# Moving regroup copies, sums and stores between engines in a linear-attention and feed-forward kernel

## The chip, the cores and the metric

The kernel runs on one core of a Trainium2 chip. The metric is the device time of one execution in microseconds (us), as the median of several runs. The core has five engines that run at the same time and wait for one another by semaphores: TensorE (PE, matrix products into the accumulator memory PSUM), VectorE (DVE), ScalarE (ACT), GpSimd (POOL), which here does copies and sums and issues the loads, and SyncE (SP), which here issues the stores. Each engine takes its own instructions in the order in which the kernel lists them.

## The reference: attention without softmax, then a feed-forward layer

```python
# q, k, v: 8 batches x 8 heads x 576 positions x 64, float32
kv  = einsum('bhsd,bhse->bhde', k, v)
att = einsum('bhsd,bhde->bhse', q, kv)
att = att / sqrt(mean(att * att, axis=-1) + 1e-6) * g_norm
x   = att.transpose(0, 2, 1, 3).reshape(4608, 512)
h   = x @ w_in                                   # 4608 x 2048
g   = maximum(h, 0) + alpha * minimum(h, 0)
out = g @ w_out                                  # 4608 x 512
```

## The kernel before

The 4608 tokens are handled in nine windows of 512 (window 0 to 8). All products are in float16 with sums in float32. While window w goes through its first layer, the attention steps of window w+1 are mixed in, and so is the second layer of window w-1.

**Loads and regroup copies.** Pool loads a batch in float16 into a staging tile. The products need k and q in another order, and a copy makes it, on Pool for batches 2 to 7 (batch 0 and 1 are copied by VectorE).

```python
def regroup(b, nm, h0, h1, eng=None):
    dst = bufs[b % NBUF][nm][:, 0:TPP, h0:h1, :].rearrange("p t h d -> p h t d")
    src = stages[b, nm][:, h0:h1, :, :]
    ...
        (eng or nc.vector).tensor_copy(out=dst, in_=src)          # L148
def regroup_batch(b):
    for nm in ("k", "q"):
        regroup(b, nm, 0, H, nc.gpsimd)
```

**Attention steps**, for four pairs of heads in each window: "t" transposes q on TensorE and copies it out of PSUM, "kv" makes the product of k and v and masks it, "ot" multiplies both and squares, "ssq" sums the squares and normalises. The results of "t" and "kv" use the same PSUM bank by turns.

```python
def step_t(b, j, pool=(ps_s, "s")):
    ...                                                           # 5 transposes, L236
    nc.vector.tensor_copy(out=qts[b, j][:], in_=qt_ps[:, 0:S])    # L245
def step_kv(b, j, pool=(ps_s, "s")):
    ...                                                           # 5 products, L251
    nc.vector.tensor_mul(out=kvs[b, j][:], in0=kv_ps[:], in1=mask32[:])   # L259
```

**First layer.** A unit of a window is one block of 128 of the 2048 columns: four products (L332), a Relu on ScalarE (L339) and a combining operation on VectorE (L343), which gives gt. A window has 16 units.

**Second layer.** For window 0 it is a plain product. From window 1 on, the four quarters of the product are computed with seven products instead of eight, from sums of activations and of weights. The activation sums s1 to s4 are made for four groups of blocks:

```python
def s_sum(w, n, k):          # a11, a21, a12, a22: quarters of the activations
    if n == 1:   nc.vector.tensor_add(out=t[:], in0=a21, in1=a22)
    elif n == 2: nc.vector.tensor_sub(out=t[:], in0=sums[w, 1, k][:], in1=a11)
    elif n == 3: nc.gpsimd.tensor_sub(out=t[:], in0=a11, in1=a21)             # L421
    else:        nc.gpsimd.tensor_sub(out=t[:], in0=a12, in1=sums[w, 2, k][:])  # L423

def w_sums(i):               # i = 0, 1; VectorE, 128x1024 each, L400 to L403
    nc.vector.tensor_sub(out=t1, in0=w_lo(i, HC, D_MODEL), in1=w_lo(i, 0, HC))
    nc.vector.tensor_sub(out=t2, in0=w_hi(i, HC, D_MODEL), in1=t1)
    nc.vector.tensor_sub(out=t4, in0=w_hi(i, 0, HC), in1=t2)
    nc.vector.tensor_sub(out=w_lo(i, HC, D_MODEL),
                         in0=w_hi(i, HC, D_MODEL), in1=w_lo(i, HC, D_MODEL))

Y_ORDER = (1, 6, 2, 7, 5, 4, 3)     # order of the seven products, 16 matmuls each (L460)
```

Product 6 reads s2, product 7 reads s3 and the fourth weight sum, product 5 reads s1, product 3 reads s4. They collect in three PSUM banks X, Y and Z; y_read (L472 to L485) adds banks and partial results together, giving the quarters c11, c22, c21 and c12, each stored when it is ready.

**The order of a window**, with what is listed for Pool in it:

```python
for w in range(1, NW):
    if 1 < w and w + 2 < B:
        load_batch(w + 2)
        regroup_batch(w + 2)                 # waits for the loads just issued
    for u in range(NF):
        if w == 1 and u == first_g - 1:      # first_g is 4 in window 1
            load_batch(3)
            regroup_batch(3)
        m1_group(w, G_ORDER[u])
        unit_sums(w, u)                      # s1, s3 and s2, s4 of a group every four units
        if w > 1 and u < 2:
            unit_sums(w - 1, NF + u)         # the last group of the window before
        ...                                  # 7 matmuls of the second layer of w-1
            if w == 1 and u == NF - 1:
                w_sums(0); w_sums(1)
        ...                                  # attention steps of w+1
```

Of the kernel before, what the change touches and what calls it, by code (L numbers as in the profile page):

```python
# [9 lines left out]
FP32 = mybir.dt.float32  # L10
FP16 = mybir.dt.float16
# [6 lines left out]
def kernel(  # L18
# [11 lines left out]
    nc = tc.nc  # L30
# [124 lines left out]
# [3 lines that stand above are left out]
# [74 lines left out]
    def step_t(b, j, pool=(ps_s, "s")):  # L232
        qs = pair_cols(b, "q", j)
        qt_ps = pool[0].tile([P, NT * P], FP16, name="qt_ps", tag=pool[1])
        for t in range(NT):
            nc.tensor.matmul(  # L236
                out=qt_ps[:, t * P : (t + 1) * P],
                lhsT=qs(t),
                rhs=ident16[:],
                is_transpose=True,  # L240
                start=(t == 0),
                stop=(t == NT - 1),
            )
        qts[b, j] = attn_p.tile([P, S], FP16, name="qt_sb", tag=f"qt{j}")
        nc.vector.tensor_copy(out=qts[b, j][:], in_=qt_ps[:, 0:S])  # L245

    def step_kv(b, j, pool=(ps_s, "s")):
        ks, vs = pair_cols(b, "k", j), pair_cols(b, "v", j)
# [107 lines left out]
    def y_mm(y, w, a, g):  # L356
# [2 lines left out]
            start=(g == 0), stop=(g == NF - 1),  # L359
        )  # L360

    def store_rows(n0, src, c0, c1):
        i = 0
        while i < P:
            b, r = divmod(n0 + i, S)
            if r < MAIN:
                t, p = divmod(r, P)
                cnt = min(P - i, P - p)
                rows = out[b * S : b * S + MAIN, :].rearrange("(p t) m -> t p m", t=TPP)
                dst = rows[t, p : p + cnt, c0:c1]  # L370
            else:
                cnt = min(P - i, S - r)
                dst = out[b * S + r : b * S + r + cnt, c0:c1]
            nc.sync.dma_start(out=dst, in_=src[i : i + cnt])
            i += cnt

    def y_out(y, w, a):
# [10 lines left out]
    def w_lo(i, c0, c1):  # L388
        return w_out_sb[i][:, :, c0:c1]

    def w_hi(i, c0, c1):
        return w_out_sb[i + WQ // 2][:, :, c0:c1]

    def w_sums(i):
        sl = slice(i * GW, (i + 1) * GW)
        for n in (1, 2, 4):
            if n not in wsum:
                wsum[n] = w_p.tile([P, NK, HC], FP16, name=f"wsum{n}")
        t1, t2, t4 = (wsum[n][:, sl, :] for n in (1, 2, 4))
        nc.vector.tensor_sub(out=t1, in0=w_lo(i, HC, D_MODEL), in1=w_lo(i, 0, HC))  # L400
        nc.vector.tensor_sub(out=t2, in0=w_hi(i, HC, D_MODEL), in1=t1)
        nc.vector.tensor_sub(out=t4, in0=w_hi(i, 0, HC), in1=t2)
        nc.vector.tensor_sub(  # L403
            out=w_lo(i, HC, D_MODEL), in0=w_hi(i, HC, D_MODEL), in1=w_lo(i, HC, D_MODEL),
        )

    sums = {}
    HW = W // 2
# [1 line left out]
    def s_sum(w, n, k):  # L410
        lo, hi = gts[w, k], gts[w, k + KQ]
        a11, a21 = lo[:, :, 0:HW], lo[:, :, HW:W]
        a12, a22 = hi[:, :, 0:HW], hi[:, :, HW:W]
        t = sum_p.tile([P, 2, HW], FP16, name=f"s{n}", tag=f"s{n}{k}", bufs=1 if n == 2 else 2)
        sums[w, n, k] = t
        if n == 1:
            nc.vector.tensor_add(out=t[:], in0=a21, in1=a22)
        elif n == 2:
            nc.vector.tensor_sub(out=t[:], in0=sums[w, 1, k][:], in1=a11)  # L419
        elif n == 3:  # L420
            nc.gpsimd.tensor_sub(out=t[:], in0=a11, in1=a21)  # L421
        else:
            nc.gpsimd.tensor_sub(out=t[:], in0=a12, in1=sums[w, 2, k][:])  # L423

    ybank = {}
    part = {}

    def y_bank(w, n):
        pool, tag = {"X": (ps_y, "y"), "Y": (ps_h, "h2"), "Z": (ps_q, "q")}[n]
        if (w, n) not in ybank:  # L430
            ybank[w, n] = pool.tile([P, 2, HC], FP32, name=f"y{n}", tag=tag)
            return ybank[w, n], True
        return ybank[w, n], False

    def prod_mm(w, n, i):
        a, c = divmod(i, NK)
        bank, fresh = y_bank(w, {1: "X", 2: "X", 6: "Y", 7: "Y", 4: "Y", 5: "Z", 3: "Z"}[n])
        cols = slice(a * P, (a + 1) * P)
        hi_cols = slice(HW + a * P, HW + (a + 1) * P)
        k, r = divmod(c, 2)  # L440
        if n == 1:
            lhs = gts[w, k][:, r, cols]
        elif n == 2:
            lhs = gts[w, k + KQ][:, r, cols]
        elif n == 4:
            lhs = gts[w, k + KQ][:, r, hi_cols]
        else:
            lhs = sums[w, {6: 2, 7: 3, 5: 1, 3: 4}[n], k][:, r, cols]
        q, rr = divmod(c, GW)
        if n == 1:  # L450
            rhs = w_out_sb[q][:, rr, 0:HC]
        elif n == 2:
            rhs = w_out_sb[q + WQ // 2][:, rr, 0:HC]
        elif n == 3:
            rhs = w_out_sb[q + WQ // 2][:, rr, HC:D_MODEL]
        elif n == 7:
            rhs = w_out_sb[q][:, rr, HC:D_MODEL]
        else:
            rhs = wsum[{4: 4, 5: 1, 6: 2}[n]][:, c, :]
        nc.tensor.matmul(  # L460
            out=bank[:, a, :], lhsT=lhs, rhs=rhs, start=fresh, stop=(i == 2 * NK - 1), skip_group_check=True,
        )

    def quad_out(w, r, h, src):
        for a in range(2):
            store_rows(w * W + r * HW + a * P, src[:, a, :], h * HC, (h + 1) * HC)

    def y_read(w, what):
        X, Y, Z = (ybank.get((w, n)) for n in "XYZ")
        if what == "p1":  # L470
            part[w, 1] = u_p.tile([P, 2, HC], FP32, name="p1")
            nc.scalar.copy(out=part[w, 1][:], in_=X[:])  # L472
        elif what in ("u2", "u3"):
            part[w, what] = u_p.tile([P, 2, HC], FP32, name=what)
            nc.vector.tensor_add(out=part[w, what][:], in0=Y[:], in1=part[w, 1][:])
        else:
            y_sb = ysb_p.tile([P, 2, HC], FP32, name="y_sb")
            if what == "c11":
                nc.scalar.copy(out=y_sb[:], in_=X[:])
            elif what == "c21":  # L480
                nc.vector.tensor_add(out=y_sb[:], in0=Y[:], in1=part[w, 1][:])
            elif what == "c22":
                nc.vector.tensor_add(out=y_sb[:], in0=Z[:], in1=part[w, "u3"][:])  # L483
            else:
                nc.vector.tensor_add(out=y_sb[:], in0=Z[:], in1=part[w, "u2"][:])  # L485
            quad_out(w, int(what[1]) - 1, int(what[2]) - 1, y_sb)

    Y_ORDER = (1, 6, 2, 7, 5, 4, 3)
    Y_LIST = [(n, i) for n in Y_ORDER for i in range(2 * NK)]
# [71 lines left out]
    def unit_sums(w, u):  # L561
        k, r = divmod(u, 4)
        k -= 1
        if k >= 0 and r < 2:
            s_sum(w, 1 if r == 0 else 2, k)
            s_sum(w, 3 if r == 0 else 4, k)

    for w in range(1, NW):
        steps = window_steps(w + 1) if w + 1 < NW else []
        n = len(steps)  # L570
        first_g = 4 if w == 1 else 0
        if w == 2:
            h_tags[0] = ("h0", "h1")
            ssq_pool[0] = (ps_s, "s")
        if 1 < w and w + 2 < B:
            load_batch(w + 2)
            regroup_batch(w + 2)
        y = None
        for u in range(NF):
            if w == 1 and u == first_g - 1:  # L580
                load_batch(3)
                regroup_batch(3)
            m1_group(w, G_ORDER[u])
            unit_sums(w, u)
            if w > 1 and u < 2:
                unit_sums(w - 1, NF + u)
            if w > 2 and u == 0:
                y_read(w - 2, "c12")
            if w == 1:
                if u == 0:  # L590
                    y = ps_y.tile([P, W], FP32, name="y_ps", tag="y")
                y_mm(y, 0, AHEAD, u)
                if u == NF - 1:
                    y_out(y, 0, AHEAD)
                    for i in range(2):
                        w_sums(i)
            else:
                for i in range(u * PER, (u + 1) * PER):
                    prod_mm(w - 1, *Y_LIST[i])
                for what in Y_READS.get(u, ()):  # L600
                    y_read(w - 1, what)

            want = n * (u - first_g + 1) // (NF - 2 - first_g)
            while steps and n - len(steps) < want:
                steps.pop(0)()
    w = NW - 1
    for u in range(NF):
        if u < 2:
            unit_sums(w, NF + u)
        if u == 0:  # L610
            y_read(w - 1, "c12")
        for i in range(u * PER, (u + 1) * PER):
            prod_mm(w, *Y_LIST[i])
        for what in Y_READS.get(u, ()):
            y_read(w, what)
    y_read(w, "c12")


# [28 lines left out]
```

## Time and profile before

| what | value |
|---|---|
| device time, median of 3 runs | 324.41 us (323.46 to 325.64) |
| span of the profiled run | 321.4 us |
| TensorE busy | 89% |
| VectorE busy | 66% |
| ScalarE busy | 45% |
| Pool busy | 44% |
| mean granted TensorE clock | 0.983 |

The profile gives for each engine how long it is busy. For groups of instructions it gives the line, the engine, what is written and read, the number, the busy time and mean duration of one in nanoseconds; behind the second bar stands the idle time of that engine just before these instructions, and what ended most of it. In the view of waits a row reads "engine, line <- releaser: us in total, times, longest". In the timeline a row begins with its start and its duration in us; a bracket at its end tells how long the engine stood idle before it, and for what.

Windows, as the timeline shows them: window 1's first layer runs from about 52.6 to 78.4 us, window 2's to 112.5, window 3's to 145.0, then about 31 to 34 us each while there is attention left to do and 28 to 30 us after that. From 301.2 us on only the second layer of window 8 is left.

### The profile page before, as it was taken

To read this page: it belongs to the slowest core of one execution; us is meant where nothing else is said; L and a number is where in the kernel's file an instruction comes from. 1 tells how busy PE (TensorE), PEld (TensorE's weight loads), DVE (VectorE), ACT (ScalarE), POOL (GpSimd) and SP (SyncE) were. 2 spreads that over 40 slices of the span, in tenths; PEclk is the share of its full clock that TensorE was granted. 3 is DMA by queue.
4 is the path that set the end of the run, shared out by engine and by line. 5 is a ranking of instruction groups with operands and counts; after the bars stand their busy time and mean duration, and the time that the engine had idled before them with its cause. 6 is when DMAs were issued, how large, how long until landed. Compare 5 with 4: busy or idle time off the path is not lost.

```text
span 321.4 us, 5167 instructions
## 1 busy us (share of the span) xinstructions
PE 285.7 (89%) x1972; PEld 179.7 (56%) x1972; DVE 211.2 (66%) x379; ACT 144.4 (45%) x240; POOL 140.1 (44%) x138
## 2 busy tenths in 40 slices
PE   5678899898499999899979997999999999999990
PEld 1424354454266666566656564656665666666780
DVE  4448844689867775677557765776777678666630
ACT  3256436466045535444445444554554556433200
POOL 8424313749645272937274726622222223432400
PEclk9799999999899999999999999999999999999997
DMA  7999999990961099107920593011102110200313
GB/s 111 184 205 196 201 196 218 104 118 34 140 82 35 8 114 198 35 4 91 213 47 2 76 206 65 7 65 35 35 0 57 44 34 17 76 8 33 100 50 82
DMA packets 52552, 28.32 MB, mean 88 GB/s; under 512 B 15136, under 2 KB 52016, under 8 KB 52528
## 3 DMA queue, kind: packets, MB, share of 16 engines
q0 software_dynamic: 40320, 18.16, 44.8%
q1 hardware_dynamic: 12208, 9.85, 11.0%
q8 instruction: 15, 0.25, 0.3%
q14 instruction: 9, 0.07, 0.1%
HBM read 36.71 MB, written 9.44 MB: 144 GB/s over the span
## 4 chain that ended last, share of the span: by engine, by line
PE 56%; DMA 10%; issue 10%; DVE 9%; POOL 9%; ACT 4%; POOLq 0%; DVEq 0%; ACTq 0%
PE h_ps L332 26%; PE yY L460 10%; PE yZ L460 7%; DMA kst<-in_k_dram 6%; DMA w_in_sb<-in_moe_w_in_dram 4%; PE yX L460 4%; DVE gt L343 3%; ACT m_sb L339 2%; PE ssq_ps L290 2%; POOL qsb L148 2%; POOL ksb L148 2%; PE kv_ps L251 2%; PE ot_ps L274 2%; POOL s L423 1%; POOL s L421 1%
## 5 line engine op out<-in xcount | busy, mean ns | idle before, releaser
L343 DVE SCALAR_TENSOR_TENSOR gt<-m_sb,beta_sb,h_ps 128x512 f16<-128x512 f32 x144 | 107.1, 745 | 65.7 <-ACT m_sb L339 64.5
L332 PE MATMUL h_ps<-xt,w_in_sb 128*128 128x512 f16 x576 | 146.9, 381 | 2.8 <-DVE gt L343 1.7
L339 ACT ACTIVATE m_sb<-h_ps 128x512 f32<-128x512 f32 x144 | 85.9, 597 | 110.5 <-PE h_ps L332 102.6
L332 PEld LDWEIGHTS <-w_in_sb 128*128 128x128 f16 x576 | 54.3, 98 | 54.9 <-issue 10.4
L423 POOL TENSOR_TENSOR s<-gt,s 128x512 f16<-128x512 f16 x32 | 37.4, 1170 | 90.1 <-DVE s L419 50.1
L460 PEld LDWEIGHTS <-s 128*128 128x128 f16 x512 | 49.9, 98 | 26.5 <-POOL s L421 5.8
L460 PEld LDWEIGHTS <-gt 128*128 128x128 f16 x384 | 37.6, 98 | 15.2 <-issue 0.6
L421 POOL TENSOR_TENSOR s<-gt 128x512 f16<-128x512 f16 x32 | 37.6, 1174 | 0.0
L460 PE MATMUL yX<-w_out_sb,gt 128*128 128x256 f16 x256 | 35.4, 274 | 0.0
L300 DVE SCALAR_TENSOR_TENSOR xt<-ot_ps,g2col,rstd 128x512 f16<-128x512 f32 x36 | 26.9, 746 | 12.9 <-ACT rstd L292 12.8
L292 ACT ACTIVATE rstd<-ssq_ps,eps_t 128x512 f32<-128x512 f32 x36 | 24.7, 687 | 17.5 <-PE ssq_ps L290 17.3
L280 ACT ACTIVATE sq_sb<-ot_ps 128x512 f16<-128x512 f32 x36 | 21.3, 596 | 23.8 <-PE ot_ps L274 23.8
L148 POOL COPY qsb<-qst 128x2048 f16<-128x2048 f16 x6 | 11.4, 1894 | 32.1 <-DMA qst<-in_q_dram 32.1
L460 PE MATMUL yY<-w_out_sb,s 128*128 128x256 f16 x128 | 19.2, 273 | 5.0 <-POOL s L421 4.9
L148 POOL COPY ksb<-kst 128x2048 f16<-128x2048 f16 x6 | 11.3, 1891 | 20.8 <-DMA kst<-in_k_dram 20.8
L290 PE MATMUL ssq_ps<-sq_sb,mask 128*128 128x512 f16 x36 | 13.6, 379 | 6.4 <-ACT sq_sb L280 4.5
L251 PEld LDWEIGHTS <-ksb 128*128 128x128 f16 x160 | 11.9, 100 | 11.6 <-issue 8.3
L251 PE MATMUL kv_ps<-vst,ksb 128*128 128x128 f16 x128 | 12.7, 225 | 6.0 <-DVE qt_sb L245 5.6
L460 PE MATMUL yZ<-w_out_sb,s 128*128 128x256 f16 x128 | 17.5, 272 | 0.3 <-DVE y_sb L483 0.2
L460 PE MATMUL yY<-wsum,s 128*128 128x256 f16 x128 | 17.6, 273 | 0.0
L460 PE MATMUL yZ<-wsum,s 128*128 128x256 f16 x128 | 17.6, 273 | 0.0
L460 PE MATMUL yY<-wsum,gt 128*128 128x256 f16 x128 | 17.6, 273 | 0.0
(64 smaller groups left out, 250.3 us busy)
## 6 DMA issues: line engine op xcount, KB each, us to landing
out_dram<-y_sb SPq DMA_DIRECT2D x80, 64.0 KB, 2.1
kst<-in_k_dram POOLq DMA_DIRECT2D x7, 512.0 KB, 7.2
qst<-in_q_dram POOLq DMA_DIRECT2D x7, 512.0 KB, 12.1
vst<-in_v_dram POOLq DMA_DIRECT2D x7, 512.0 KB, 9.9
out_dram<-y_sb SPq DMA_DIRECT2D x24, 128.0 KB, 2.0
w_in_sb<-in_moe_w_in_dram POOLq DMA_DIRECT2D x4, 512.0 KB, 15.2
w_out_sb<-in_moe_w_out_dram POOLq DMA_DIRECT2D x4, 512.0 KB, 16.0
out_dram<-y_sb SPq DMA_DIRECT2D x4, 256.0 KB, 2.8
```

The source lines that it names most:

```text
L148: (eng or nc.vector).tensor_copy(out=dst, in_=src)
L251: nc.tensor.matmul(out=kv_ps[:], lhsT=ks(t), rhs=vs(t), start=(t == 0), stop=(t == NT - 1),)
L280: nc.scalar.activation(out=sq[:], in_=ot_ps[:], func=AF.Square)
L290: nc.tensor.matmul(out=ssq_ps[:], lhsT=mask16[:], rhs=sq[:], start=True, stop=True)
L292: nc.scalar.activation(out=rstd[:], in_=ssq_ps[:], func=AF.Abs_reciprocal_sqrt, bias=eps_t[:], scale=inv_d,)
L300: nc.vector.scalar_tensor_tensor(out=xts[w, j][:], in0=ot_ps[:], scalar=g2col[:], in1=rstd[:], op0=ALU.mult, op1=ALU.mult,)
L332: nc.tensor.matmul(out=h_ps[:], lhsT=w_in_blk(c, g), rhs=xts[w, c][:], start=(c == 0), stop=(c == NC - 1),)
L339: nc.scalar.activation(out=m_sb[:], in_=h_ps[:], func=AF.Relu, scale=-1.0)
L343: nc.vector.scalar_tensor_tensor(out=gts[w, i][:, r, :], in0=m_sb[:], scalar=beta_sb[:, g : g + 1], in1=h_ps[:], op0=ALU.mult, op1=ALU.add,)
L421: nc.gpsimd.tensor_sub(out=t[:], in0=a11, in1=a21)
L423: nc.gpsimd.tensor_sub(out=t[:], in0=a12, in1=sums[w, 2, k][:])
L460: nc.tensor.matmul(out=bank[:, a, :], lhsT=lhs, rhs=rhs, start=fresh, stop=(i == 2 * NK - 1), skip_group_check=True,)
```

## The change

It moves work between the engines and along Pool's order; what is computed stays the same.

- **Regroup copies later.** The k and q copies for batch w+2 are listed behind the sums of units 10 and 12 of window w, and no longer right behind their loads. The loads of batch 3 move from unit 3 of window 1 to its start (Pool has nothing listed in between).
- **Activation sums.** s4 goes from Pool to VectorE from window 2 on and is listed one unit later. Pool keeps s3.
- **q copies** out of PSUM go from VectorE to ScalarE for batches 1 to 7.
- **Weight sums** go from VectorE to Pool. Six of the eight are listed at the start of window 1 behind the loads of batch 3, the last two at the start of window 2.
- **Last sum in two banks.** In window 8, the two halves of bank Z lie in two PSUM banks, and c12 is summed and stored in two halves, the first while the second is still being multiplied.
- **Stores on two queues.** In the last stage the stores go by turns to SyncE's and ScalarE's queues.

The aim is that Pool's queue no longer stands behind a load, that VectorE has less to do where the second layer starts, and that the end of the run is shorter. The diff, cut to its core:

```diff
 def step_t(...):
-        nc.vector.tensor_copy(out=qts[b, j][:], in_=qt_ps[:, 0:S])
+        if b == 0:
+            nc.vector.tensor_copy(out=qts[b, j][:], in_=qt_ps[:, 0:S])
+        else:
+            nc.scalar.copy(out=qts[b, j][:], in_=qt_ps[:, 0:S])
 def store_rows(...):
-            nc.sync.dma_start(out=dst, in_=src[i : i + cnt])
+            engs = store_engines[0]
+            store_turn[0] += 1
+            engs[store_turn[0] % len(engs)].dma_start(out=dst, in_=src[i : i + cnt])
-    def w_sums(i):                       # four nc.vector.tensor_sub
+    def w_sum(n, i):                     # one nc.gpsimd.tensor_sub, n = 1, 2, 4 or 3
 def s_sum(...):
-            nc.gpsimd.tensor_sub(out=t[:], in0=a12, in1=sums[w, 2, k][:])
+            eng = nc.gpsimd if w == 1 else nc.vector
+            eng.tensor_sub(out=t[:], in0=a12, in1=sums[w, 2, k][:])
 def y_bank(w, n, a):
+        if w == NW - 1 and n == "Z":     # one bank for each half
+            key = (w, n, a)
+            if a == 1:
+                pool, tag = ps_h, "h1"
 def unit_sums(w, u):
-        if k >= 0 and r < 2:
-            s_sum(w, 1 if r == 0 else 2, k)
-            s_sum(w, 3 if r == 0 else 4, k)
+        if k >= 0 and r < 3:
+            s_sum(w, (1, 2, 4)[r], k)
+            if r == 0:
+                s_sum(w, 3, k)
 for w in range(1, NW):
+            for i in range(2):           # in window 2 only
+                w_sum(3, i)
-        if 1 < w and w + 2 < B:
+        if 0 < w and w + 2 < B:
             load_batch(w + 2)
-            regroup_batch(w + 2)
+        if w == 1:
+            for i in range(2):
+                for m in (1, 2, 4):
+                    w_sum(m, i)
         for u in range(NF):
-            if w == 1 and u == first_g - 1:
-                load_batch(3)
-                regroup_batch(3)
             m1_group(w, G_ORDER[u])
             unit_sums(w, u)
-            if w > 1 and u < 2:
+            if w > 1 and u < 3:
                 unit_sums(w - 1, NF + u)
+            if w + 2 < B and u in (10, 12):
+                regroup(w + 2, "k" if u == 10 else "q", 0, H, nc.gpsimd)
-                    for i in range(2):
-                        w_sums(i)
 w = NW - 1
+store_engines[0] = (nc.sync, nc.scalar)
 for u in range(NF):
             prod_mm(w, *Y_LIST[i])
+            if i == len(Y_LIST) - NK - 1:
+                y_read(w, "c12", (0,))
-    y_read(w, "c12")
+    y_read(w, "c12", (1,))
```

## The prediction

> **What bounds the kernel now.** I read the page's busy shares first, then the view of waits, then the timeline of each long wait. Three lines of the page set the scene:
>
> ```profile
> PE 285.7 (89%) x1972; PEld 179.7 (56%) x1972; DVE 211.2 (66%) x379; ACT 144.4 (45%) x240; POOL 140.1 (44%) x138
> ...
> L423 POOL TENSOR_TENSOR s<-gt,s 128x512 f16<-128x512 f16 x32 | 37.4, 1170 | 90.1 <-DVE s L419 50.1
> ...
> L148 POOL COPY qsb<-qst 128x2048 f16<-128x2048 f16 x6 | 11.4, 1894 | 32.1 <-DMA qst<-in_q_dram 32.1
> ```
>
> TensorE (PE) is busy for 89% of the span, so only its gaps are to be won. Pool (POOL) is 44% busy, but its copies stand idle for a DMA, and everything behind them in its queue stands too. The waits say when TensorE is the one that pays:
>
> ```profile
> PEld L460 <- POOL s L421: 5.8, 3, 2.3
> PE kv_ps L251 <- DVE qt_sb L245: 5.6, 3, 4.6
> ...
> PE yY L460 <- POOL s L421: 4.9, 3, 2.0
> ```
>
> Three waits for Pool's sum s3 cost TensorE 4.9 us (the weight-load row is the same three waits), and one wait for a VectorE (DVE) copy cost 4.6 us. The timeline explains both. At the second wait for s3:
>
> ```profile
> 162.49 1.89 POOL L148 COPY qsb<-qst 128x2048 f16<-128x2048 f16 x1 [5.69 <-DMA qst<-in_q_dram]
> ...
> 164.34 1.14 POOL L421 TENSOR_TENSOR s<-gt 128x512 f16<-128x512 f16 x1
> ...
> 165.54 0.39 PE L460 MATMUL yY<-w_out_sb,s 128*128 128x256 f16 x2 [1.77 <-POOL s L421]
> ```
>
> The q copy waited 5.69 us for its load; the last s3 of the window stood behind it in Pool's order, and product 7 needs it. The same happens at 132.25 (1.14 us) and 199.08 (2.01 us): 1.14 + 1.77 + 2.01 = 4.92 us.
>
> The other wait is the eight weight sums on VectorE at the start of window 2:
>
> ```profile
> 78.64 1.27 DVE L400 TENSOR_TENSOR wsum<-w_out_sb 128x1024 f16<-128x1024 f16 x1
> ...
> 83.94 0.68 DVE L403 TENSOR_TENSOR w_out_sb<-w_out_sb,w_out_sb 128x1024 f16<-128x1024 f16 x1
> 84.54 0.74 DVE L343 SCALAR_TENSOR_TENSOR gt<-m_sb,beta_sb,h_ps 128x512 f16<-128x512 f32 x1
> 85.20 0.42 DVE L417 TENSOR_TENSOR s<-gt 128x512 f16<-128x512 f16 x1
> 85.53 0.45 DVE L245 COPY qt_sb<-qt_ps 128x576 f16<-128x576 f16 x1
> ...
> 86.03 0.58 PE L251 MATMUL kv_ps<-vst,ksb 128*128 128x128 f16 x4 [4.64 <-DVE qt_sb L245]
> ```
>
> VectorE is in order, so the q copy (L245) waits behind them, and TensorE behind the copy. Afterwards its clock is low: the matmul group at 86.52 takes 1.91 us where the usual one takes 1.03, and it recovers near 88.65. Of those 2.6 us about half, 1.3 us, is lost.
>
> The end of the run is the third place. SyncE issues the last twelve stores one after the other:
>
> ```profile
> 310.99 7.50 SPq L374 DMA_DIRECT2D out_dram<-y_sb  x12
> ...
> 313.76 0.69 DVE L485 TENSOR_TENSOR y_sb<-yZ,u 128x512 f32<-128x512 f32 x1 [1.05 <-PE yZ L460]
> ```
>
> 12 in 7.50 us is 0.625 us each. The last sum is done at 314.45, but the issuing ends at 318.49, and the span at 321.4, 2.9 us later.
>
> **What the Trainium skill says.** (1) "SBUF — State Buffer", section "SBUF: two separate sides": GpSimd and a VectorE instruction with two SBUF inputs share a port pair under an exclusive lock; the later one stands until the first is through. The trace agrees: the VectorE sum L417 at 93.70 takes 1.88 us instead of 0.42 and gets through only after a Pool copy (93.41 to 95.30). (2) "GPSIMD Engine Reference", "Performance versus the Vector engine": two-input arithmetic is about twice as slow there as on VectorE, one-input copies are not held back so. Here it is worse: 1.155 us against 0.418 for the same 128x512 sum, 2.8 times. (3) "TensorE: Matmul & The Clock Gate", "What's actually happening": after a window of idleness (about 3.4 us) the clock falls to half and takes about as long to return. The 4.64 us gap and the doubled matmuls agree. (4) "DMA: Bandwidth & Descriptors", "Issuing engines are not separate DMA queues": a second issuing engine saves only the issuing time. That is just what the tail is made of, though no run here has issued from ScalarE yet.
>
> **The change, part by part.**
>
> *Regroup copies later and s4 on VectorE (windows 2 to 8).* From window 2 on, Pool keeps one sum of four: four of 1.155 us a window instead of eight. The k and q copies go behind the sums of units 10 and 12, some 20 us after their loads are issued; the loads land in 7 to 12 us. So s3 no longer stands behind a load: **-4.9 us**. VectorE gains 28 sums of 0.42 (11.8 us) and loses 28 q copies of 0.45 (12.6) and the weight sums (6.1 with the first one's wait), so it doesn't become the bound. ScalarE gains 28 copies; a 128x512 copy from PSUM takes 0.58 there, so I put 0.64 on 576 columns: 18 us, 45% to 50% busy. A q copy has some 3.7 us between its transpose and the kv product that reuses its bank. I count nothing for it.
>
> *Weight sums on Pool.* These leave VectorE, and the 4.64 us wait with its slow clock would go. But see what Pool must do before window 2. Its q copy for batch 2 ends at 56.98 and the six load issues for batch 3 at 61.61, as before. Then come six weight sums of 128x1024. I have no row for this on Pool; twice the 1.11 us pitch of back-to-back 512-column sums gives 2.2 us each, 13.3 together: 74.9. Some five VectorE sums will take the port in between, and a Pool sum that meets one takes 1.33 instead of 1.15: +1, 75.9. Next in order: four activation sums (4.5), the k copy (1.9), one sum (1.1), the q copy (1.9): 9.4. **The q copy of batch 3 is done near 85.4**, where it was done at 72.3 before. TensorE wants it at the transpose at 79.33, the first step of window 2. So a wait of about 6 us replaces one of 4.64, and the clock falls again. How the two compare: the kv product follows the transpose by 2.06 us of TensorE work (79.33 to 81.39, where its wait began), so it comes at 85.4 + 0.2 for the handshake + 2.06 = 87.7, where it came at 86.03: **+1.7 us**. What VectorE loses to Pool's lock in window 1 only makes TensorE arrive later at a wait that Pool sets anyway.
>
> Is there a second wait behind it? After the q copy: one sum, two weight sums (4.4), six issues (4.7), then s3 for the last group, near 97. Product 7 gets to it at unit 7.7 of window 2, about 85.6 + 7.7 x 1.95 + 1.3 = 101.9. It fits. VectorE's sums will meet the long Pool sums there, though: **+0.4 us**, from one earlier collision of this kind that cost TensorE 0.79 at 95.83.
>
> *The end.* TensorE's last product of sixteen matmuls ends where it did. Its first half is now in its own bank and is summed near 313.05. From a 512-column sum of 0.685 with about 1.04 ns a column I take 0.42 for 256. VectorE's order is now first half, c21, second half: 313.47, 314.15, 314.57. The stores on two queues: c22's four from 310.99, two each; the first half's two, one each from 313.5; c21's four, two each from 314.2, until 315.45; the last two, one each, until 316.08. Against 318.49 that is **-2.4 us**, if ScalarE issues as fast as SyncE. ScalarE has no work left there.
>
> Sum: -4.9 + 1.7 + 0.4 - 2.4 = -5.2. From the 324.41 us median: **319.2 us, ratio 0.984.**
>
> **The rivals.** *The weight sums are nearly free on Pool.* Then the wait at 79.33 doesn't come, the 4.64 + 1.3 goes, and the sum is -4.9 - 5.9 - 2.4 = -13.2, 311 us. For it: in window 1 Pool is idle 2.17 + 4.74 us before its copies. Against: 13.3 us don't fit into 6.9, and they stand ahead of the copies. *The port lock is the bound.* VectorE is stopped for up to 2.2 us by each of six long Pool sums in window 1, and again in window 2; in window 1 it is hidden under the wait, but if the collisions go on in later windows at the 0.79 us seen, two a window for five windows would take back some 8 us: 327. Against: s3 is ready two units before its VectorE neighbours, so the two mostly pass each other. *The q copies on ScalarE delay the next Relu.* Each 0.64 us there, if the two PSUM banks have no room, costs up to 28 x 0.2 = 5.6 us: 325. Against: ScalarE waits for TensorE before most of its Relus.
>
> **The range and the chances.** The Pool chain is the largest term and rests on an estimated duration: 2.0 or 2.5 us a sum moves it by -1 or +2. The tail could be worth 1.5 to 2.7. Collisions may cost 0 to 3. That gives 315.0 to 323.0. The 2% line is 317.9, only 1.3 us below my value, so faster by over 2% has 0.36, within 2% 0.58, slower 0.06.
>
> **What would show it.** In the changed profile: no TensorE wait for s from window 3 on; Pool weight sums of about 2.2 us from 61.6 to about 76; the q copy of batch 3 ending near 85.5 with one TensorE wait of about 6 us before the transposes of window 2, and a low clock after it; the last issue on either queue near 316. A q copy done before 80, or a wait missing there, would make me too high; new waits of TensorE for VectorE in windows 3 to 6 would make me too low.

## The result and the profile after

| | before | after |
|---|---|---|
| device time, median (lowest to highest), us | 325.02 (323.46 to 326.58) | 316.08 (316.08 to 316.11) |
| ratio | 1 | **0.9725**, 95% interval 0.9675 to 0.9775 |
| span of the profiled run, us | 321.4 | 314.3 |

Predicted was 319.2. The profiled run of the kernel before is the fastest of its runs, so the two traces differ by 7.1 us where the medians differ by 8.9. All that follows explains the 7.1.

First the page of the kernel after: the busy shares, and the groups that changed engine.

```profile
PE 287.0 (91%) x1972; PEld 180.7 (57%) x1972; DVE 219.3 (70%) x373; ACT 161.1 (51%) x268; POOL 127.2 (40%) x118
...
L437 POOL TENSOR_TENSOR s<-gt 128x512 f16<-128x512 f16 x32 | 39.1, 1223 | 134.5 <-DVE gt L346 134.2
...
L248 ACT COPY qt_sb<-qt_ps 128x576 f16<-128x576 f16 x28 | 17.9, 638 | 15.3 <-PE qt_ps L236 15.3
L440 DVE TENSOR_TENSOR s<-gt,s 128x512 f16<-128x512 f16 x28 | 21.2, 758 | 0.0
```

L437 is s3, from window 2 on the one activation sum left on Pool. Pool now waits for VectorE's gt before it, and for no load. No row of the waits names TensorE waiting for a sum of Pool any more. L440 is s4 on VectorE: 758 ns on the mean, where a VectorE sum that nothing stops takes 420. In window 3, for example, two of the four took 0.42 us, and the two beside the k and the q copy 1.30 and 1.64.

The view by stretches shows where the 7.1 us came from. Its columns are the stretch, its length, the busy time of PE, PEld, DVE, ACT and POOL with counts, the granted TensorE clock, the DMA share and GB/s. First the kernel before (the first layer of window 1, then all of window 3), then the same two of the kernel after with window 2 between them:

```profile
52.60:78.40 25.80, 22.98 (x137) 11.39 (x136) 19.10 (x34) 16.08 (x28) 16.40 (x15) 1.00 0.72 104
112.31:144.97 32.66, 30.72 (x228) 20.50 (x228) 22.54 (x42) 15.64 (x26) 17.62 (x16) 1.00 0.60 90
```

```profile
52.40:85.00 32.60, 26.32 (x137) 12.34 (x136) 22.64 (x30) 18.41 (x32) 29.52 (x21) 0.90 0.57 85
85.00:113.24 28.24, 26.51 (x202) 17.72 (x202) 24.39 (x35) 16.16 (x28) 24.21 (x22) 1.00 0.74 95
113.24:144.33 31.09, 30.39 (x228) 20.60 (x228) 24.26 (x42) 18.01 (x30) 13.41 (x12) 1.00 0.63 92
```

Window 1 got 6.8 us longer: 32.60 against 25.80 us for the same 137 matmuls, at a clock of 0.90 instead of 1.00. TensorE's busy time in window 1 grew by 3.3 us, which goes with the lower clock (26.32 against 22.98), its idle time by 3.5 (6.28 against 2.82). Window 3 got 1.6 us shorter. Taken from mark to mark (the last ssq product of one window to that of the next), windows 3 to 6 took 32.66, 33.30, 33.53 and 31.35 us before and 31.09, 31.16, 31.17 and 31.16 after.

The timeline of window 1 shows Pool's weight sums (L407 to L419) and what becomes of VectorE beside them:

```profile
70.54 2.18 POOL L411 TENSOR_TENSOR wsum<-w_out_sb,wsum 128x1024 f16<-128x1024 f16 x1
71.33 1.68 DVE L435 TENSOR_TENSOR s<-s,gt 128x512 f16<-128x512 f16 x1
...
72.93 0.28 DVE L262 TENSOR_TENSOR kv_sb<-kv_ps,mask 128x128 f16<-128x128 f32 x1
...
73.26 0.44 PE L236 MATMUL qt_ps<-ident,qsb 128*128 128x128 f16 x5 [1.73 <-DVE kv_sb L262]
...
82.69 1.89 POOL L148 COPY qsb<-qst 128x2048 f16<-128x2048 f16 x1
...
85.82 0.44 PE L236 MATMUL qt_ps<-ident,qsb 128*128 128x128 f16 x5
```

Pool's sum runs from 70.54 to 72.72. VectorE's sum s2, 0.42 us of work, starts at 71.33 and ends at 73.01, just behind it. The mask of the kv product (L262) stands behind s2 in VectorE's order, and the next transpose reuses that bank: TensorE stood for 1.73 us. Other gaps end at 62.27 (2.67 us), 78.87 (1.16) and 79.89 (0.68). The gap of 1.16 comes from s1 on VectorE, which starts at 77.20 beside Pool's s3 (77.18) and takes 1.42 us. The one of 2.67 begins with an s1 of 1.95 us beside Pool's load issues. The gap of 0.68 isn't new: TensorE waited 0.68 us for the same step before the change, at 74.99. The last row shown is the start of window 2, at 85.82: it has no bracket. TensorE came there later than Pool's q copy, which was done at 82.69 + 1.89 = 84.58.

The end of the run:

```profile
302.20 8.34 SPq L382 DMA_DIRECT2D out_dram<-y_sb  x8
302.20 8.65 ACTq L382 DMA_DIRECT2D out_dram<-y_sb  x8
...
308.64 0.42 DVE L516 TENSOR_TENSOR y_sb<-yZ,u 128x256 f32<-128x256 f32 x1
```

The last product ends at 308.54, the last half sum at 309.06, the last issue at 310.85 on ScalarE's queue, the span at 314.3.

### The profile page after: what moved, and what is told of

It reads as the page before. It is cut to its first block, busy times and chain, and to the rows that moved or that the text cites. A ratio compares the mean times of both kernels' runs of the same rounds, so it can differ in the third digit from the quotient of the medians.

```text
span 314.3 us, 5166 instructions
## 1 busy us (share of the span) xinstructions
PE 287.0 (91%) x1972; PEld 180.7 (57%) x1972; DVE 219.3 (70%) x373; ACT 161.1 (51%) x268; POOL 127.2 (40%) x118
## 4 chain that ended last, share of the span: by engine, by line
PE 76%; DVE 12%; ACT 5%; issue 2%; DMA 2%; SPq 1%; DVEq 0%
PE h_ps L335 34%; PE yY L486 11%; PE yZ L486 9%; PE yX L486 7%; DVE gt L346 4%; PE qt_ps L236 3%; DVE s L433 3%; ACT m_sb L342 3%; PE ot_ps L277 3%; PE ssq_ps L293 2%; PE kv_ps L254 2%; DMA alpha_row<-in_moe_alpha_dram 2%; DVE s L435 1%; ACT sq_sb L283 1%; DVE y_sb L513 1%
## 5 line engine op out<-in xcount | busy, mean ns | idle before, releaser
L335 PE MATMUL h_ps<-xt,w_in_sb 128*128 128x512 f16 x576 | 148.9, 384 | 2.2 <-DVE gt L346 1.4
L437 POOL TENSOR_TENSOR s<-gt 128x512 f16<-128x512 f16 x32 | 39.1, 1223 | 134.5 <-DVE gt L346 134.2
L248 ACT COPY qt_sb<-qt_ps 128x576 f16<-128x576 f16 x28 | 17.9, 638 | 15.3 <-PE qt_ps L236 15.3
L440 DVE TENSOR_TENSOR s<-gt,s 128x512 f16<-128x512 f16 x28 | 21.2, 758 | 0.0
L236 PE MATMUL qt_ps<-ident,qsb 128*128 128x128 f16 x160 | 14.5, 226 | 6.0 <-DVE kv_sb L262 5.2
L433 DVE TENSOR_TENSOR s<-gt 128x512 f16<-128x512 f16 x32 | 18.8, 588 | 0.0
L236 PEld LDWEIGHTS <-qsb 128*128 128x128 f16 x160 | 11.8, 101 | 9.8 <-issue 5.9
```

Source lines behind the costliest of these rows:

```text
L236: nc.tensor.matmul(out=qt_ps[:, t * P : (t + 1) * P], lhsT=qs(t), rhs=ident16[:], is_transpose=True, start=(t == 0), stop=(t == NT - 1),)
L335: nc.tensor.matmul(out=h_ps[:], lhsT=w_in_blk(c, g), rhs=xts[w, c][:], start=(c == 0), stop=(c == NC - 1),)
L440: eng.tensor_sub(out=t[:], in0=a12, in1=sums[w, 2, k][:])
```

## The experiments

**Theory A:** Pool's order, weight sums ahead of the regroup copies of batch 3, holds the start of window 2 (the prediction's view). **Theory B:** the port that VectorE's sums share with Pool stretches window 1 by itself. The first three kernels separate the two. The diffs are shortened.

### 1. Weight sums in window 0

```diff
-    regroup_batch(2)
+    w_sum(1, 0); w_sum(1, 1); w_sum(2, 0)
+    regroup(2, "k", 0, H, nc.gpsimd)
+    w_sum(4, 0); w_sum(2, 1)
+    regroup(2, "q", 0, H, nc.gpsimd)
     if w == 1:          # was: all six
+        w_sum(4, 1)
```

> Five of the six early weight sums stand in window 0, in the times where Pool waits for the loads of batch 2; one stays at the start of window 1. Both theories of the loss before window 2 (the port lock, and Pool's chain up to the q copy of batch 3) are taken away at once. Expected: window 1's units are 1.6 us or less apart again, the transpose of window 2 starts near 79 instead of 85.8 us, and the time falls by 5.5 to 7.5 us, to 308.5 to 310.5 us. If the loss has another cause (the q copies on ScalarE, the later loads), the time stays near 316.

Measured: 315.35 us, ratio 0.9724 (0.9656 to 0.9792), 0.7 us below the change where 5.5 to 7.5 were expected. Window 2 starts at 86.78 and not near 79. Hardly anything of Theory A's chain is left here, since five of the six sums are gone from window 1; but the one that stayed was enough. Its timeline:

```profile
61.35 2.53 DVE L435 TENSOR_TENSOR s<-s,gt 128x512 f16<-128x512 f16 x1
61.44 2.15 POOL L415 TENSOR_TENSOR wsum<-w_out_sb,wsum 128x1024 f16<-128x1024 f16 x1
...
64.14 0.69 PE L236 MATMUL qt_ps<-ident,qsb 128*128 128x128 f16 x5 [4.38 <-DVE kv_sb L262]
```

s1 had already taken 1.53 us beside the load issues. s2 takes 2.53 us against Pool's 2.15, and TensorE stands for 4.38 us and works at a low clock afterwards. Later the q copy, now free to start early (77.41, 1.89 us), stops VectorE's s1 at 77.47 for 2.10 us, which costs 1.85 us of TensorE and the clock again. This speaks for B.

### 2. The chain without the lock

Experiment 1, with 23 fills of an unused tile on Pool behind the one weight sum that it left in window 1. They take Pool's time and read nothing.

```diff
         w_sum(4, 1)
+        for i in range(23):
+            nc.gpsimd.memset(warm16[:], 0.5)
```

> As e1, but Pool fills about the time of the other five weight sums at the start of window 1 with 23 fills of a constant into a dead tile, which read nothing. So Pool's chain up to the q copy of batch 3 is about as long as in the changed kernel, without sums that read. Theory 'the chain sets it anyway': VectorE's sums keep their 0.42 us, TensorE comes to the transpose of window 2 near 79 us and waits there until the q copy is done near 84, one gap of about 5 us, time 315 to 317 us. Theory 'only the lock costs': TensorE goes on at 79, time 308.5 to 310.5 us.

Measured: 318.25 us, ratio 0.9817 (0.9726 to 0.9907). From its timeline:

```profile
63.20 13.33 POOL L621 MEMSET warm<- 128x512 f16 x23
...
68.70 0.42 DVE L433 TENSOR_TENSOR s<-gt 128x512 f16<-128x512 f16 x1
...
84.23 1.89 POOL L148 COPY qsb<-qst 128x2048 f16<-128x2048 f16 x1
...
86.18 0.72 PE L236 MATMUL qt_ps<-ident,qsb 128*128 128x128 f16 x5 [5.09 <-POOL qsb L148]
```

VectorE's sums keep their 0.42 us beside the fills (at 68.70, 70.28 and 74.89), TensorE arrives at 81.09, and then it stands for 5.09 us for the q copy, just as the prediction described it for the change. So Theory A's chain is real: where the lock is taken away, the chain sets the start of window 2, at 86.18. The chain is somewhat longer here than in the change: its q copy ends at 86.12, there at 84.58.

### 3. The lock without the chain

The kernel after, with the k and q copies of batch 3 on ScalarE, so that they stand behind no weight sum.

```diff
-                regroup(w + 2, "k" if u == 10 else "q", 0, H, nc.gpsimd)
+                regroup(w + 2, "k" if u == 10 else "q", 0, H, nc.scalar if w == 1 else nc.gpsimd)
```

> The changed kernel with the k and q copies of batch 3 on ScalarE: Pool's weight sums still meet VectorE's sums in window 1, but the q copy doesn't stand behind them. Theory 'the lock stretches window 1': gaps of TensorE for VectorE's mask (2.7 and 1.7 us) stay, the transpose of window 2 starts after 83 us, time 314 to 317 us. Theory 'only the chain': it starts near 79 to 80, time 309 to 311 us.

Measured: 313.04 us, ratio 0.9656 (0.9569 to 0.9743). From its timeline:

```profile
72.99 0.44 PE L236 MATMUL qt_ps<-ident,qsb 128*128 128x128 f16 x5 [2.13 <-DVE kv_sb L262]
...
79.62 0.38 PE L293 MATMUL ssq_ps<-sq_sb,mask 128*128 128x512 f16 x1 [0.69 <-ACT sq_sb L283]
...
83.95 0.44 PE L236 MATMUL qt_ps<-ident,qsb 128*128 128x128 f16 x5
```

Window 2 starts at 83.95, with no wait for the q copy. TensorE's gaps for VectorE's mask are still there (3.13 us at 61.98, 2.13 at 72.99, 1.16 at 78.59). With these copies off Pool's chain, window 1 still ends 4.6 us later than the 79.33 of before. Its last ssq product, at 79.62, comes 0.27 us before that of the kernel after (79.89), so up to there the chain had cost hardly anything. Most of the 1.9 us between the two starts of window 2 arises behind that product, where this kernel ran at the full clock and the kernel after at half.

**Both limits hold at nearly the same place.** In the kernel after the chain is done at 84.58, and the lock alone leads to 83.95 here. Experiments 7 and 10, which are the kernel after up to the end of window 1, show how close the two are: there TensorE came at 83.24 and 83.08, and it did wait for the q copy, 0.87 and 1.12 us. This is the row of experiment 10:

```profile
84.20 0.45 PE L236 MATMUL qt_ps<-ident,qsb 128*128 128x128 f16 x5 [1.12 <-POOL qsb L148]
```

### 4. Weight sums back on VectorE

The kernel after, with all eight weight sums on VectorE at the end of window 1, as before.

```diff
-            nc.gpsimd.tensor_sub(...)        # in w_sum, all four
+            nc.vector.tensor_sub(...)
+                    for i in range(2):       # at the last unit of window 1
+                        for m in (1, 2, 4, 3):
+                            w_sum(m, i)
```

> The changed kernel with all eight weight sums back on VectorE at the end of window 1. If moving them to Pool was worth about nothing, as the trace suggests (6.5 us lost in window 1 against 4.64 us and a slow clock of 1.3 us saved): 314.5 to 317 us, with the wait of 4.6 us for VectorE at the start of window 2 back. If the move carried the gain: 321 to 323 us.

Measured: 316.19 us, ratio 0.9755 (0.9695 to 0.9816), against 316.08 with them on Pool. Window 2 starts at 81.54 and TensorE then waits 4.00 us for VectorE's gt at 87.88. The move of the weight sums, the largest part of the change to look at, was worth about nothing: it took one wait away and gave window 1 others. With the sums on VectorE, window 1 isn't free of stops either: the q copy on Pool in its later place (72.16, 1.89 us) stops VectorE's s1 for 2.11 us, and TensorE waits 1.85 us behind it.

### 5. All sums of window 1 on Pool

If B is right, sums that are on Pool themselves can't be stopped by Pool. Early weight sums as in experiment 1, s1 to s4 of window 1 on Pool, the last early weight sum behind the copies at unit 10, and the two that are left on VectorE in window 2.

```diff
-            nc.vector.tensor_add(out=t[:], in0=a21, in1=a22)          # s1; s2 likewise
+            (nc.gpsimd if w == 1 else nc.vector).tensor_add(out=t[:], in0=a21, in1=a22)
+            if w == 1 and u == 10:
+                regroup(3, "k", 0, H, nc.gpsimd)
+                regroup(3, "q", 0, H, nc.gpsimd)
+                w_sum(4, 1)
+            if w == 2 and u == 3:
+                w_sum(3, 0); w_sum(3, 1)     # on VectorE
```

> As e1, and in window 1 all four activation sums are on Pool, so that VectorE has no sum of two SBUF inputs that Pool can stop; the k and q copies of batch 3 and the one remaining weight sum follow unit 10's sums; the fourth weight sums (0.7 us each) are on VectorE in window 2. Lock theory: no TensorE gap over 1 us in window 1, the transpose of window 2 starts at 78 to 80 us, time 308.5 to 311 us. If window 1 is stretched by something else (q copies on ScalarE, the kv mask itself), its gaps stay and the time is 313 or more.

Measured: 314.91 us, ratio 0.9705 (0.9657 to 0.9753), where 308.5 to 311 us were expected. Window 1 itself behaved nearly as expected: its longest gap is 1.18 us, and window 2 starts at 77.94. But the gain went into a new wait, as the timeline shows:

```profile
85.17 0.92 POOL L131 DMA_DIRECT2D qst<-in_q_dram  x1
86.06 1.34 POOL L433 TENSOR_TENSOR s<-gt 128x512 f16<-128x512 f16 x1
...
88.48 1.14 POOL L435 TENSOR_TENSOR s<-s,gt 128x512 f16<-128x512 f16 x1
...
89.68 1.46 PE L486 MATMUL yY<-wsum,s 128*128 128x256 f16 x6 [6.52 <-POOL s L435]
```

The sums of the last group are listed in window 2, behind the six load issues of batch 4. These ran from 81.35 to 86.09, and the sum s2, which product 6 reads, was done at 89.62. TensorE stood for 6.52 us.

### 6. The later regroup copies alone

The kernel before, with only the loads of batch 3 and all regroup copies moved.

```diff
-        if 1 < w and w + 2 < B:
+        if 0 < w and w + 2 < B:
             load_batch(w + 2)
-            regroup_batch(w + 2)
-            if w == 1 and u == first_g - 1:
-                load_batch(3)
-                regroup_batch(3)
+            if w + 2 < B and u in (10, 12):
+                regroup(w + 2, "k" if u == 10 else "q", 0, H, nc.gpsimd)
```

> The kernel before with nothing but the later place of the k and q copies (and of the loads of batch 3). The waits for s3 in windows 3 to 5 should go. By TensorE's own row they are 4.9 us, by the weight loads' row 5.8: 318.5 to 320 us if these waits are the whole gain there, 315 to 317 us if the copies' order carries nearly all of the change, 323 us if s4's move to VectorE is what freed Pool.

Measured: 323.57 us, ratio 0.9995 (0.9967 to 1.0023): no gain. That is the number of the third case expected, but not its reason: TensorE's waits for s3 are gone, without s4's move, and windows 3 to 5 take 32.05 us each, 3.3 less in sum than before. But each of these windows has a new gap; one of them in the timeline:

```profile
142.48 1.89 POOL L148 COPY qsb<-qst 128x2048 f16<-128x2048 f16 x1
143.53 1.12 DVE L417 TENSOR_TENSOR s<-gt 128x512 f16<-128x512 f16 x1
144.57 0.68 DVE L483 TENSOR_TENSOR y_sb<-yZ,u 128x512 f32<-128x512 f32 x1
145.30 0.38 PE L460 MATMUL yZ<-w_out_sb,s 128*128 128x256 f16 x2 [0.71 <-DVE y_sb L483]
```

The q copy in its new place stops VectorE's s1 until 144.65, the sum that empties bank Z comes later, and product 3 waits 0.71 us for that bank. Windows 1 and 2 lose another 2.2 us: the same meeting of q copy and s1 at 72.75, with a gap of 1.72 us at 75.19, and a wait for the weight sums of 5.88 us at 88.49, longer than the 4.64 of before.

### 7. One store queue

```diff
-    store_engines[0] = (nc.sync, nc.scalar)
+    store_engines[0] = (nc.sync,)
```

> The changed kernel with the last stores on SyncE alone; the halves of the last sum stay. If the second queue makes the shorter end: 1.5 to 2.2 us slower than the changed kernel, 317.5 to 318.3 us. If the halved sum makes it: within 0.5 us of 316.1.

Measured: 317.07 us, ratio 0.9772 (0.9697 to 0.9847). The end of its timeline:

```profile
301.32 10.90 SPq L382 DMA_DIRECT2D out_dram<-y_sb  x16
...
307.77 0.41 DVE L516 TENSOR_TENSOR y_sb<-yZ,u 128x256 f32<-128x256 f32 x1
```

Windows 1 and 2 were 0.9 us shorter in this kernel than in the one after, which has nothing to do with the stores, so the ends are compared from the last sum on. Here it is 6.92 us from 308.18 to the end at 315.1, after the change 5.24. **The second queue is worth 1.7 us**, more than the 1.0 between the medians.

### 8. q copies back on VectorE

```diff
-        if b == 0:
-            nc.vector.tensor_copy(out=qts[b, j][:], in_=qt_ps[:, 0:S])
-        else:
-            nc.scalar.copy(out=qts[b, j][:], in_=qt_ps[:, 0:S])
+        nc.vector.tensor_copy(out=qts[b, j][:], in_=qt_ps[:, 0:S])
```

> The changed kernel with the q copies out of PSUM on VectorE for all batches. In windows 3 to 8 nothing should change (31.2 us each, VectorE isn't the bound). In window 1 the copies would stand behind stopped sums, so TensorE gets a new wait for qt_sb there, 0 to 2 us: 316 to 318 us. If ScalarE's copies are what stretched window 1: 313 to 315 us.

Measured: 319.97 us, ratio 0.9861 (0.9786 to 0.9937), 3.9 us slower than after and above everything expected. Its waits have a row that the kernel after lacks:

```profile
PE kv_ps L251 <- DVE qt_sb L245: 7.8, 10, 1.8
```

Windows 3 to 5 take 32.01, 32.16 and 32.15 us, where 31.2 was expected. In each of them s4 on VectorE meets the k copy on Pool (at 132.16 it takes 1.30 us), the q copy out of PSUM stands behind it, and the kv product waits 0.50 us for that. In windows 4 and 5 a second wait for a q copy, of 0.17 us, is added.

### 9. Experiment 5 with the last group's s1 and s2 on VectorE

Experiment 5 shows what is in the way, so this takes it out: the two sums that stood behind the load issues go back to VectorE.

```diff
-            (nc.gpsimd if w == 1 else nc.vector).tensor_add(out=t[:], in0=a21, in1=a22)
+            (nc.gpsimd if w == 1 and k < 3 else nc.vector).tensor_add(out=t[:], in0=a21, in1=a22)
```

> As e5, with the two sums s1 and s2 of window 1's last group back on VectorE, since in e5 they came behind six load issues on Pool and TensorE waited 6.5 us for them in window 2. If that wait was only a matter of Pool's order: the transpose of window 2 starts near 78 us as in e5, window 2 has no gap above 1.5 us, and the time is 6 to 8 us below e5's 314.9, 306.5 to 309 us. If the lock strikes again where Pool's sums of group 2 meet VectorE's two: up to 2.5 us of gap, 309 to 311.5 us.

Measured: **307.61 us, ratio 0.9488 (0.9442 to 0.9534)**, the fastest of all, 8.5 us below the change. Its busy shares:

```profile
PE 283.3 (93%) x1972; PEld 180.3 (59%) x1972; DVE 211.6 (69%) x369; ACT 160.6 (52%) x268; POOL 129.5 (42%) x122
```

And its window 1 in the view by stretches:

```profile
52.60:77.10 24.50, 22.41 (x137) 11.31 (x136) 15.10 (x24) 17.90 (x32) 23.57 (x20) 1.00 0.76 110
```

Window 1 takes 24.50 us at the full clock instead of 32.60 at 0.90. Pool is occupied for nearly all of it (23.57 of 24.50, with the load issues), and VectorE's part fell from 22.64 to 15.10. From there on the windows are those of the change (31.09 to 31.17 us), so nearly all of the gain is made by the start of window 2, at 78.03 instead of 85.82: 7.8 us.

### 10. s4 back on Pool

```diff
-            eng = nc.gpsimd if w == 1 else nc.vector
+            eng = nc.gpsimd
```

> The changed kernel with s4 on Pool in all windows. e6 had the late copies with s4 on Pool and q copies on VectorE and lost 0.71 us a window at product 3, because the q copy ran behind s4 and met VectorE's s1. If s4's move is what avoids that meeting: windows 3 to 6 take 31.8 to 32.1 us each and not 31.2, and the time is 2 to 4 us above 316.1. If the q copies on ScalarE alone avoid it: windows of 31.2 us and 316 us.

Measured: 316.91 us, ratio 0.9779 (0.9718 to 0.984). Windows 3 to 5 are as expected, 31.79 us each, with the 0.71 us gap of experiment 6 back. The total isn't: windows 1 and 2 came out 1.3 us shorter, as they also did by 0.9 in experiment 7. Window 1 is the same code in these two kernels and in the one after, but it didn't run the same: VectorE's sums met Pool's for other lengths of time, and both kernels had one stretch of half clock in it (from about 77 and 78 us), where the kernel after had two. So totals that lie 1 us apart say little, and the windows are the better measure.

Windows 3 to 5 of experiments 6, 8 and 10 and of the kernel after make a table of two moves (all four have the copies in their later place; experiment 6 lists s4 one unit earlier than the others):

| us a window | s4 on Pool | s4 on VectorE |
|---|---|---|
| q copies on VectorE | 32.05 (experiment 6) | 32.0 to 32.2 (experiment 8) |
| q copies on ScalarE | 31.79 (experiment 10) | 31.09 to 31.17 (after) |

Neither move alone brings more than 0.3 us. Both together bring 0.9. The waits that stay in the other three show why: with the q copies still on VectorE, they stand behind a stopped s4 (experiment 8), and with s4 still on Pool, the q copy runs later, stops s1, and the sum that empties bank Z comes late (experiments 6 and 10).

## Why the prediction was right on the whole and wrong in a step

The total lay 3.1 us below what was predicted, inside the range. Its terms, from the marks in the two traces:

| step | predicted, us | measured, us |
|---|---|---|
| windows 3 to 6: the waits for s3 go | -4.9 | -6.3 |
| start of window 2, first kv product | +1.7 | +1.7 (87.72 against 86.03) |
| rest of window 2: collisions | +0.4 | -0.8 (25.52 us against 26.28) |
| windows 7, 8 and the last stage | 0 | +0.15 |
| after the last product | -2.4 | -1.9 (5.76 us against 7.68) |
| sum | -5.2 | -7.1 |

**The waits for s3: right, with a term missing.** They went as described. But the copies in their new place alone bring 3.3 us in windows 3 to 5 (experiment 6), less than the 4.9, since they stop VectorE instead. The rest comes from the q copies on ScalarE, of which the prediction said "I count nothing for it", together with s4 on VectorE: 0.9 us in each of three windows. The estimated 0.64 us for the copy was right (638 ns), and the rival that it would delay the Relus is refuted: without the move the kernel takes 3.9 us more (experiment 8).

**The start of window 2: the right number for the wrong reason.** Predicted was a kv product at 87.7, behind a TensorE wait of about 6 us for a q copy done near 85.4. The q copy was done at 84.58, the kv product came at 87.72, and the wait didn't exist. The step that failed is the sentence that what VectorE loses to the lock in window 1 "only makes TensorE arrive later at a wait that Pool sets anyway". It made TensorE arrive later than that wait. The time was lost inside window 1: 3.5 us more of idle time, in three gaps that are new or longer than before (2.67, 1.73 and 1.16 us), and 3.3 us more of busy time, with two stretches at half clock. Only the gap of 1.73 lies beside a weight sum; the one of 1.16 lies beside Pool's s3, and the one of 2.67 begins beside load issues, whose part stays open (last section). Experiment 3 shows that this loss remains without the chain, and experiment 2 that the chain was the hidden second limit; in the kernel after its q copy was ready 85.82 - 84.58 = 1.24 us before TensorE came. The step failed by little: in experiments 7 and 10, the same code up to there with one stretch of half clock less, TensorE came first and the wait existed, at 0.87 and 1.12 us instead of the 6 foretold. The rival "the port lock is the bound" named the right mechanism and put it into the wrong windows: for window 1 it had it hidden under the wait, and it looked for the loss in five later windows, where it costs TensorE almost nothing (it is busy for 30.39 of the 31.09 us of window 3), though s4's 758 ns instead of 420 show it.

**Window 2: wrong sign.** The prediction had the clock fall at the start of window 2. It fell in window 1, and window 2 ran at 1.00, so the 1.3 us that it had lost there before came back. Taken from the prediction's own 1.3, the collisions would then cost about 0.5 us, near the 0.4 expected; no run shows this by itself.

**The end: right in the issuing, mis-sized behind it.** The last issue was expected 316.08 - 313.72 = 2.36 us after the last product and came 310.85 - 308.54 = 2.31 after it. But from the last issue to the end it is 3.45 us, where SyncE's queue alone needs 2.9 (before, and in experiment 7). This took back 0.5 of the 2.4.

**Where the gain could have been larger.** The chances leaned to within 2% because the time up to window 2's kv product was thought to be lost on either engine. Experiment 4 confirms that much: the weight sums on either engine give the same time. Experiment 9 shows that this loss wasn't needed.

## What to carry to other kernels

Before work is moved to GpSimd, look at what VectorE does meanwhile: the two-input sums of VectorE that met a long GpSimd sum or copy in the rows above got through only when that one had ended, and what stands behind it in VectorE's order pays, so put dependent short sums on the same engine as the long ones or keep the two apart in time. When a wait is taken away, work out every limit at that place and not only the one that comes last, since a second one may lie within 2 us of it: taking the copies out of the chain brought 3.0 us (experiment 3), while freeing the chain and the stopped sums together brought 8.5 (experiment 9). Judge a small part by the stage it works in: two moves that bring 0.3 us or less each can bring 0.9 together, and the total may hide it.

## What the runs showed of the hardware

- **What the lock stops.** The Trainium skill, "SBUF — State Buffer", section "SBUF: two separate sides", says that a VectorE operation with two SBUF inputs contends only with a GpSimd operation that reads SBUF. The runs agree: a sum took 0.42 us beside the fills of experiment 2, but 1.68 us beside a weight sum in the kernel after and 2.53 in experiment 1.
- **A short gap can be enough for the clock, and the same gap isn't always.** The skill's "TensorE: Matmul & The Clock Gate", section "What's actually happening", speaks of an idle window of about 3.4 us. The measured gaps are shorter: in the kernel after, one of 2.67 us and two of 1.16 and 0.68 us that lie close together were followed by half clock. But one of 2.40 us in experiment 10 and the pair of 1.16 and 0.69 us in experiment 3 were not, so no length of gap in these runs tells by itself whether the clock falls. Nor does the mean clock tell the time: the four runs of the kernel after lie within 0.03 us at mean clocks of 0.973 to 0.991. The view by stretches of the kernel after (columns as above; 0.50 and 0.51 are the clock):

```profile
64.40:66.40 2.00, 2.00 (x8) 0.73 (x7) 0.75 (x1) 0.86 (x2) 1.92 (x2) 0.50 1.49 189
...
80.00:82.00 2.00, 2.00 (x6) 0.74 (x5) 2.00 (x3) 0.69 (x1) 2.00 (x2) 0.51 0.00 0
```

- **An open point.** The first s1 of window 1 on VectorE, near 59 us, runs beside Pool's load issues, not beside a sum. It took 1.95 us in the kernel after and 1.3 to 2.4 in the six others in which a weight sum stands directly behind those issues in Pool's order (experiments 1, 2, 3, 7, 8 and 10), but 0.42 before, where a copy that waits for its load stands there, and in experiments 4 and 6, where s3 does. Where it is slow it ends about 0.2 us after the last issue starts. This is the beginning of the 2.67 us gap. The cause wasn't found; none of these runs takes the issues away and leaves the sum.
